# Who copies the dense half tiles, and when the third sequence's z is transposed, in a fused attention and mixture-of-experts kernel

## The chip, the cores and the metric

The kernel runs on one core of a Trainium2 chip. The metric is device time in microseconds (us) of one execution of the whole program, lower is better. The engines are called as in the profile: PE is TensorE (PEld its weight loads), DVE is VectorE, ACT is ScalarE, POOL is GpSimd, SP is SyncE, which here only issues DMAs.

## The reference

```python
B, S, D = u.shape                              # 8, 2816, 256; z has 64 columns
scores = (1 / S) * (z @ z.T)                   # per sequence; symmetric
attn = np.maximum(scores, 0) ** 2
x = (u * (attn @ v)).reshape(B * S, D)         # 22528 tokens
h = np.maximum(x @ w1_dense, 0)                # 512 hidden columns
y_dense = h @ w2_dense
expert = argmax(x @ w_gate)                    # one of 8 experts per token
gate = softmax(x @ w_gate)[expert]
y_moe[token] = gate * (np.maximum(x @ w1[expert], 0) @ w2[expert])
out = y_dense + y_moe
```

## The kernel before, in words

The program has two stages on one core.

**Stage one, attention.** Each of the 8 sequences is 22 blocks of 128 tokens. The columns of A = relu(scores)^2 are made in groups of 2 or 4 blocks, six groups to a sequence: PE computes scores into PSUM (`scores`, L408), ACT or DVE applies relu (L423 or L425) and then the square (L436 or L438), which writes the tile A in SBUF. A has three buffers. Because A is symmetric, some blocks of a group are not computed but taken from an earlier group by a DMA transpose that SP issues (`far_steps`, L493, seen as `A<-A` and `wall<-A`); the buffer of that earlier group can be written again when these transposes have read it. PE then multiplies A by v (`av`, L610), two blocks at a time, and DVE multiplies the result by u (`gate_x`, L637): one L637 per two blocks. DVE also routes (small operations, L681 to L741), and POOL scatters the tokens of a block to per-expert rows in DRAM (L779).

The scores need z transposed. For the first sequence this is done by PE. For every other sequence `turn_z` does it in two halves of 11 blocks: a DVE copy that doubles z (L115, `zn<-zr`) and a DMA transpose on SP's queue (L118, `zT<-zn`). SP's queue is served in order; it also carries the loads of u (L154), the transposes of x for the routing (L639) and those of L493.

The order of the instructions on PE, ACT, DVE and SP is written out when the program is built: a small planner keeps a clock of its own (`now`) and the times at which it believes ACT, DVE and SP's queue to be free, and puts each operation on an engine by these. `tick(g)` is called once per block. `soon(t, fn, dur)` offers a piece of DVE work at tick t with a duration that the planner charges; `issue(1.5)` charges SP's queue for a transpose of z. A group's scores may be started two groups ahead (`ahead`), but those of another sequence only when both halves of its z are in the program (`z_there`).

**Stage two, experts.** The tokens come back from DRAM sorted by expert. The first region has NT1 = 70 tiles of 256 tokens, each tile of one expert; the second region has units of two half tiles of 128 tokens, each half with an expert of its own. A tile is two halves. Per tile, in PE's order (`slot`):

- `up` with the dense weights (L1003, `h_ps<-ring,w1d`, 8 matmuls), and its relu on ACT (L1006)
- `half(s - 2, 1)`: the second half of the tile before the last
- `up` with the expert's weights, and its relu on ACT
- `half(s - 1, 0)`: the first half of the last tile

In between, DVE copies the expert's weights for the next tile to a ring (L990, one copy of 128x2048 per tile in the first region, two per unit in the second). A `half` is: eight matmuls (`down`, L1012) into the tile `y`, four of them for the dense part `y[:, 0]` and four for the expert's part `y[:, 1]`; a copy of the dense part from PSUM to the SBUF tile `yd` by ACT (L1029); one DVE instruction that multiplies the expert's part by the gate, adds `yd` and writes `ys` (L1030); and an indirect DMA from POOL's queue that writes the rows of `ys` to the output (L1032). After some of them POOL does a small copy that only spaces its DMAs (L1017). `y` has two buffers, each a PSUM bank; `h_ps` has three, `yd` three, `ys` nine. PE can write a buffer of `y` again when its L1030 is done. Some of the last scatters of stage one and the tables of the second region (16 steps on DVE, one for each tile from the eleventh on, L821 to L906) are done between the tiles.

Of the kernel before, what the change touches and what calls it, by code (L numbers as in the profile page):

```python
# [19 lines left out]
def kernel(  # L20
# [12 lines left out]
    nc = tc.nc  # L33
# [6 lines left out]
    nK = S // P  # L40
# [9 lines left out]
    NT1 = -(-(Q1 * G * P - E * (T2 - 1)) // T2)  # L50
# [53 lines left out]
    def load_z(b):  # L104
        z_of[b] = zpool.tile([P, nK, dq], BF, name="zr", bufs=1)
        nc.vector.memset(z_of[b][:, 0, 0:1], 0.0)
        nc.gpsimd.dma_start(out=z_of[b][:], in_=z[b].rearrange("(p k) d -> p k d", p=P))

    def turn_z(b, k0, k1):

        if k0 == 0:
            assert not any(left[m] for m in left if groups[m][0] == b - 2)
            zn_of[b] = zpool.tile([P, nK, 2, dq], BF, name="zn", bufs=1)
            zT_of[b] = zpool.tile([P, nK, P], BF, name="zT")
        nc.vector.tensor_copy(  # L115
            zn_of[b][:, k0:k1, :, :],
            z_of[b][:, k0:k1, :].unsqueeze(2).to_broadcast([P, k1 - k0, 2, dq]))
        nc.sync.dma_start_transpose(  # L118
            out=zT_of[b][:, k0:k1, :],
            in_=zn_of[b][:, k0:k1].rearrange("p k h d -> p (k h d)"))  # L120
        issue(1.5)
        if k1 == nK:
            z_there.add(b)

    def load_v(b, h, parts, gate=True):
        if h == 0:
            v_of[b] = zpool.tile([P, nK, D], BF, name="vb")
        src = v[b].rearrange("(p k) d -> p k d", p=P)
        k0, k1 = h * nK // parts, (h + 1) * nK // parts
        if gate:  # L130
            nc.vector.memset(v_of[b][:, k0, 0:1], 0.0)
        nc.gpsimd.dma_start(out=v_of[b][:, k0:k1, :], in_=src[:, k0:k1, :])
        free["pool"] = max(free["pool"], now[0]) + 0.8
# [12 lines left out]
    def issue(dur, ready=0.0):  # L146
        sync[0] = max(sync[0], now[0], ready) + dur
# [114 lines left out]
    def weights(e, half):  # L262
        nc.vector.memset(wall[:, e, half * 2 * F:half * 2 * F + 1], 0.0)
        if half == 0:
            nc.gpsimd.dma_start(
                out=wall[:, e, 0:2 * F].rearrange("p (c f) -> p c f", c=2),
                in_=moe_w1[e].rearrange("(c p) f -> p c f", p=P))
        else:
            nc.gpsimd.dma_start(
                out=wall[:, e, 2 * F:].rearrange("p (c d) -> p c d", c=4),  # L270
                in_=moe_w2[e].rearrange("(c p) d -> p c d", p=P))
# [20 lines left out]
    def offer(ready, rank, ways, then=None):  # L292
        count[0] += 1
        todo.append((rank, count[0], ready, ways, then))
# [120 lines left out]
    def relu(n, ks, s, c, ready, sx):  # L415
# [39 lines left out]
        if n + ks[0] == 0:  # L455
            del ways["act"]
        offer(ready, 1, ways, half)

    def can_turn(n, m):
# [287 lines left out]
    def nodep(ins, mine, *groups_):  # L747
        ins = ins.ins if hasattr(ins, "ins") else ins
        for key in groups_:
            tc.declare_no_dep(ins, group=key, reason="rows of different tokens")  # L750
        for key in mine:
            tc.add_to_no_dep_group(key, ins)
# [3 lines left out]
    def behind(fn):  # L756

        if last_pool:
            with tc.issue_after(last_pool[0]):
                ins = fn()  # L760
        else:
            ins = fn()
        last_pool[:] = [ins.ins]
        return ins
# [172 lines left out]
    def take(name):  # L937
        if not ring:
            rings()
        turn[name] = turn.get(name, -1) + 1  # L940
        return ring[name][turn[name] % len(ring[name])]
# [68 lines left out]
    def down(y, k, h, w2, j):  # L1010
        for f in range(4):
            nc.tensor.matmul(out=y[:, k, :], lhsT=h[:, f, j * P:(j + 1) * P],  # L1012
                             rhs=w2(f), start=(f == 0), stop=(f == 3))

    def pause(src):

        behind(lambda: nc.gpsimd.tensor_copy(take("idle")[:, :src.shape[1]], src))  # L1017
# [3 lines left out]
    def half(s, j):  # L1021

        hd, he, we, me, ids = pend[s]
        we = we[j % len(we)]
        yd, ys = take("yd"), take("ys")
        y = late["y"].tile([P, 2, D], F32, name="yy", tag="y")
        down(y, 0, hd, lambda f: w2d[:, f, :], j)
        down(y, 1, he, lambda f: we[:, 2 * F + f * D:2 * F + (f + 1) * D], j)
        nc.scalar.copy(yd, y[:, 0, :])  # L1029
        nc.vector.scalar_tensor_tensor(out=ys, in0=y[:, 1, :], scalar=me[:, j, 0:1],  # L1030
                                       in1=yd, op0=ALU.mult, op1=ALU.add)
        ins = behind(lambda: nc.gpsimd.indirect_dma_start(  # L1032
            out=out, out_offset=bass.IndirectOffsetOnAxis(ap=ids[j], axis=0),
            in_=ys, in_offset=None, bounds_check=N - 1, oob_is_err=False))
        nodep(ins, ["out"], "out")
        last_row[0] = ins
        if j == 0 and s < NT - MAYBE - 5:
            pause(ys)
# [16 lines left out]
    def slot(s, end):  # L1055

        def second_half():
            if s - 2 in pend:
                if halves(s - 2) == 2:
                    half(s - 2, 1)  # L1060
                del pend[s - 2]
# [33 lines left out]
    def at(tick, fn):  # L1095
        later.setdefault(tick, []).append(fn)

    def soon(t, fn, dur=0.07):
        at(t, lambda: offer(now[0], 3, {"dve": (dur, lambda eng: fn())}))
# [8 lines left out]
    for b in range(B):  # L1108
        t = b * nK
        if b + 1 < B:  # L1110
            soon(max(t - 10, 0), lambda b=b: load_z(b + 1))
            soon(t - 1 if b else 5, lambda b=b: turn_z(b + 1, 0, nK // 2), 0.4)
            soon(t if b else 6, lambda b=b: turn_z(b + 1, nK // 2, nK), 0.4)
            for h in range(2):
                soon(t + (13, 15)[h], lambda b=b, h=h: load_v(b + 1, h, 2))

# [69 lines left out]
    for q in range(nQ - 2):  # L1186
        t = starts[q + 1] - 1 + LAG
# [93 lines left out]
```

## Time and profile before

| what | value |
|---|---|
| three runs | 905.21, 912.65 and 927.82 us, median 912.65 |
| the profiled execution, its own time | 910.9 us |
| its span, first to last instruction | 909.2 us (1.7 us lie around it) |
| mean granted TensorE clock | 0.992 |
| stage one, stage two | about 566 and 343 us of the span |

One execution was profiled. The page gives each engine's busy time and the idle time in front of its instructions with the instruction that ended it ("releaser"). In the views of time each row begins with its start and its duration in us; `x8` is a count of merged instructions, and a bracket at the end says how long the engine sat idle before and what released it. Views by windows give busy time per stretch, with the number of instructions behind an x, then the granted clock (PEclk, 1.00 is full), the share of the DMA engines and GB/s. Ends of matmuls are modelled: eight matmuls of 256 columns are listed with 1.04 us and the next eight begin 0.87 us after them.

### The profile page before, as it was taken

The page shows a single profiled execution, that of the slowest core. Times are in us where ns is not written, and L with a number is a line of the kernel's source. Part 1 is how long each engine was busy: PE and PEld are TensorE (multiplying, and loading weights), DVE is VectorE, ACT ScalarE, POOL GpSimd, SP SyncE. Part 2 cuts the span into 40 slices and gives each one's busy share as a digit, 9 for nine tenths or more (in the row PEclk, how much of TensorE's full clock was granted, in tenths as well). Part 3 has the DMA queues.
Part 4 walks back from the last instruction along what each step waited for, and adds up shares of the span by engine and source line. Part 5 has one row for each costly group of instructions (what it writes and reads, how often), then busy time and mean ns, then how long its engine had stood idle before and what let it go on. Part 6 is the DMA issues. An engine that isn't in the chain of part 4 may idle for free.

```text
span 909.2 us, 30147 instructions
## 1 busy us (share of the span) xinstructions
PE 865.5 (95%) x12178; PEld 757.4 (83%) x12178; DVE 669.7 (74%) x1275; ACT 702.9 (77%) x873; POOL 486.0 (53%) x538
## 2 busy tenths in 40 slices
PE   7999897999999999999999999899999999999996
PEld 5898796898898898788898878688887888888885
DVE  8989695898997998897998985545654444546663
ACT  8989695897897897797897984566766776777664
POOL 7202343244344344344244374778787887777765
PEclk9999999999999999999999999999999999999999
DMA  8998999999999999999999867555544544544333
GB/s 175 174 199 152 179 175 133 172 196 199 194 190 174 200 177 163 192 204 180 200 170 179 148 143 135 118 123 113 113 113 108 115 111 115 112 102 102 92 94 86
DMA packets 289246, 136.80 MB, mean 150 GB/s; under 512 B 258638, under 2 KB 266062, under 8 KB 289104
## 3 DMA queue, kind: packets, MB, share of 16 engines
q1 hardware_dynamic: 263552, 79.40, 52.4%
q0 software_dynamic: 25552, 55.44, 27.4%
q8 instruction: 96, 1.57, 0.7%
q14 instruction: 46, 0.38, 0.1%
HBM read 61.54 MB, written 37.03 MB: 108 GB/s over the span
## 4 chain that ended last, share of the span: by engine, by line
PE 62%; POOL 15%; issue 12%; DVE 5%; DMA 3%; ACT 2%; POOLq 0%; another core or an unknown queue 0%; DVEq 0%; ACTq 0%
PE o L610 41%; POOL out_dram L1032 11%; PE s L408 9%; PE yy L1012 5%; PE h_ps L1003 5%; POOL zr L1017 3%; DMA wall<-A 1%; DVE r L425 1%; PE lg L671 1%; DMA vb<-in_v_dram 1%; ACT A L436 1%; DVE pays L637 1%; DVE ring L1030 1%; DVE A L438 1%; ACT r L423 1%
## 5 line engine op out<-in xcount | busy, mean ns | idle before, releaser
L610 PE MATMUL o<-vb,A 64*128 64x256 bf16 x7184 | 464.4, 270 | 8.5 <-issue 5.8
L610 PEld LDWEIGHTS <-A 64*128 64x128 bf16 x7184 | 381.5, 94 | 51.3 <-issue 10.7
L779 POOL DMA_INDIRECT xs<-pays,pi x176 | 189.1, 1075 | 281.2 <-DVE pi L777 232.5
L423 ACT ACTIVATE r<-s 128x1024 f32<-128x1024 f32 (+1 forms) x246 | 242.5, 1010 | 50.3 <-PE s L408 48.0
L436 ACT ACTIVATE A<-r 128x1024 bf16<-128x1024 f32 (+1 forms) x246 | 248.7, 1042 | 8.7 <-issue 3.1
L1006 ACT ACTIVATE ring<-h_ps 128x1024 bf16<-128x1024 f32 x180 | 184.6, 1026 | 90.8 <-PE h_ps L1003 51.7
L425 DVE TENSOR_SCALAR r<-s 128x1024 f32<-128x1024 f32 x151 | 182.8, 1219 | 14.3 <-PE s L408 12.4
L1030 DVE SCALAR_TENSOR_TENSOR ring<-yy,me,ring 128x256 f32<-128x256 f32 x179 | 86.3, 482 | 141.4 <-ACT ring L1029 70.9
L438 DVE TENSOR_TENSOR A<-r 128x1024 bf16<-128x1024 f32 x145 | 175.3, 1218 | 3.8 <-ACT r L423 2.8
L1032 POOL DMA_INDIRECT out_dram<-ring,me x140 | 145.5, 1039 | 54.9 <-DVE ring L1030 27.2
L1012 PEld LDWEIGHTS <-ring 128*128 128x128 bf16 x1432 | 139.3, 98 | 34.9 <-issue 17.1
L408 PE MATMUL s<-zT 64*128 64x512 bf16 (+1 forms) x874 | 146.9, 357 | 7.7 <-ACT r L423 2.4
L1012 PE MATMUL yy<-w2d,ring 128*128 128x256 bf16 x716 | 107.8, 273 | 12.2 <-DVE ring L1030 11.6
L1012 PE MATMUL yy<-ring 128*128 128x256 bf16 x716 | 107.9, 273 | 2.4 <-ACT ring L1006 1.4
L1003 PE MATMUL h_ps<-ring,w1d 128*128 128x256 bf16 x720 | 93.7, 274 | 2.6 <-ACT ring L1006 2.6
L1003 PE MATMUL h_ps<-ring 128*128 128x256 bf16 (+1 forms) x872 | 93.5, 253 | 0.6 <-ACT ring L1006 0.6
L990 DVE COPY ring<-wall 128x2048 bf16 x109 | 82.9, 775 | 11.6 <-issue 7.1
L637 DVE TENSOR_TENSOR pays<-o,ut 128x512 bf16<-128x512 f32 x88 | 60.2, 684 | 38.7 <-PE o L610 16.9
L1029 ACT COPY ring<-yy 128x256 f32<-128x256 f32 x179 | 67.3, 376 | 23.2 <-PE yy L1012 11.4
L1003 PEld LDWEIGHTS <-ring 128*128 128x128 bf16 x872 | 73.5, 98 | 8.5 <-issue 1.2
L1003 PEld LDWEIGHTS <-w1d 128*128 128x128 bf16 x720 | 70.2, 98 | 11.2 <-issue 2.9
L408 PEld LDWEIGHTS <-zT 64*128 64x128 bf16 x874 | 54.7, 94 | 23.9 <-issue 11.2
(124 smaller groups left out, 448.2 us busy)
## 6 DMA issues: line engine op xcount, KB each, us to landing
ut<-in_u_dram SPq DMA_DIRECT2D x88, 256.0 KB
vb<-in_v_dram POOLq DMA_DIRECT2D x14, 704.0 KB
wall<-in_moe_w_dram POOLq DMA_DIRECT2D x16, 256.0 KB
xs<-pays,pi POOLq DMA_INDIRECT x176
zr<-in_z_dram POOLq DMA_DIRECT2D x7, 352.0 KB
out_dram<-ring,me POOLq DMA_INDIRECT x140
ring<-xs SPq DMA_TRANSPOSE x114
xT<-pays SPq DMA_TRANSPOSE x88
```

What stands on the lines that cost most here:

```text
L408: nc.tensor.matmul(out=s[:, h, y * c:(y + 1) * c], lhsT=zT[r, k + h, :], rhs=zT[r, i0:i0 + w, :], start=True, stop=True)
L423: nc.scalar.activation(r[:, :, :c], s[:, :, :c], AF.Relu, scale=1.0 / S)
L425: nc.vector.tensor_scalar(out=r[:, :, :c], in0=s[:, :, :c], scalar1=1.0 / S, scalar2=0.0, op0=ALU.mult, op1=ALU.max)
L436: nc.scalar.activation(a, r, AF.Square)
L438: (nc.gpsimd if eng == "pool" else nc.vector).tensor_mul(a, r, r)
L610: nc.tensor.matmul(out=o[:, j, 0:D], lhsT=block(n, k, i + j - i0)[r], rhs=v_of[b][r, k, :], start=(p == 0 and x == 0), stop=(p == 1 and x ...
L779: ins = behind(lambda: nc.gpsimd.indirect_dma_start(out=xs, out_offset=bass.IndirectOffsetOnAxis(ap=pi[:], axis=0), in_=pays[:, g % (2 * G ...
L1003: nc.tensor.matmul(out=h_ps[:, f, hs, :], lhsT=w1(c, f), rhs=xT[:, hs, c, :], start=(c == 0), stop=(c == 1))
L1006: nc.scalar.activation(h[:, :, 0:m * P], h_ps[:, :, 0:m, :].rearrange("p f h t -> p f (h t)"), AF.Relu)
L1012: nc.tensor.matmul(out=y[:, k, :], lhsT=h[:, f, j * P:(j + 1) * P], rhs=w2(f), start=(f == 0), stop=(f == 3))
L1030: nc.vector.scalar_tensor_tensor(out=ys, in0=y[:, 1, :], scalar=me[:, j, 0:1], in1=yd, op0=ALU.mult, op1=ALU.add)
L1032: ins = behind(lambda: nc.gpsimd.indirect_dma_start(out=out, out_offset=bass.IndirectOffsetOnAxis(ap=ids[j], axis=0), in_=ys, in_offset=No ...
```

## The change

```diff
@@ half(s, j) @@
-        nc.scalar.copy(yd, y[:, 0, :])
+        if s < NT1:
+            nc.vector.tensor_copy(yd, y[:, 0, :])
+        else:
+            nc.scalar.copy(yd, y[:, 0, :])
         nc.vector.scalar_tensor_tensor(out=ys, in0=y[:, 1, :], scalar=me[:, j, 0:1],
                                        in1=yd, op0=ALU.mult, op1=ALU.add)
@@ the list of what is offered at which tick; t = b * nK, nK = 22 @@
         if b + 1 < B:
             soon(max(t - 10, 0), lambda b=b: load_z(b + 1))
-            soon(t - 1 if b else 5, lambda b=b: turn_z(b + 1, 0, nK // 2), 0.4)
-            soon(t if b else 6, lambda b=b: turn_z(b + 1, nK // 2, nK), 0.4)
+            tz = (5, 6) if b == 0 else (t + 9, t + 11) if b == 1 else (t - 1, t)
+            soon(tz[0], lambda b=b: turn_z(b + 1, 0, nK // 2), 0.4)
+            soon(tz[1], lambda b=b: turn_z(b + 1, nK // 2, nK), 0.4)
```

In the first region (140 half tiles) the copy of the dense part goes from ACT to DVE; in the second region (39 half tiles) it stays on ACT. The two halves of `turn_z` for the third sequence (b = 1) are offered at ticks 31 and 33 in place of 21 and 22; for the other sequences the ticks are as before. Nothing else changes in the source, but the planner sees the moved work at its new place.

## The prediction

> **What bounds the kernel now.** I read the page first, then the windows by stage, then the timelines of the two places that the change touches.
>
> ```profile
> PE 865.5 (95%) x12178; PEld 757.4 (83%) x12178; DVE 669.7 (74%) x1275; ACT 702.9 (77%) x873; POOL 486.0 (53%) x538
> PE 62%; POOL 15%; issue 12%; DVE 5%; DMA 3%; ACT 2%; POOLq 0%; another core or an unknown queue 0%; DVEq 0%; ACTq 0%
> ```
> ```profile
> 0.00:566.00 566.00, 546.65 (x9147) 475.59 (x9148) 485.01 (x885) 472.62 (x513) 226.67 (x242) 0.99 1.02 176
> 586.50:825.40 238.90, 229.66 (x2082) 203.10 (x2080) 123.39 (x244) 167.21 (x261) 187.78 (x216) 1.00 0.48 113
> 825.40:909.20 83.80, 72.91 (x810) 65.45 (x807) 49.74 (x102) 51.46 (x84) 57.10 (x62) 0.98 0.37 92
> ```
>
> The columns after the length are PE, PEld, DVE, ACT and POOL. PE is the bound in all stretches, busy 95% overall and 96% in the first region (second row, tiles 5 to 69). So a change pays only where PE stands still, and costs only where it makes PE stand still. I therefore looked for PE's gaps at the two places.
>
> Place one is the second sequence, ticks 22 to 34:
>
> ```profile
> 86.50 3.72 SPq L118 DMA_TRANSPOSE zT<-zn  x2
> 91.46 2.25 SPq L493 DMA_TRANSPOSE wall<-A  x1
> 95.45 2.22 SPq L493 DMA_TRANSPOSE wall<-A  x1
> 103.25 1.06 ACT L436 ACTIVATE A<-r 128x1024 bf16<-128x1024 f32 x1 [3.04 <-DMA wall<-A]
> 105.27 0.61 PE L408 MATMUL s<-zT 64*128 64x512 bf16 x4 [2.38 <-ACT r L423]
> ```
> ```profile
> 100.00:120.00 20.00, 17.55 (x259) 13.98 (x255) 14.98 (x28) 15.48 (x18) 5.91 (x5) 0.91 0.93 163
> 120.00:140.00 20.00, 19.91 (x364) 18.42 (x360) 17.05 (x31) 16.57 (x20) 10.59 (x12) 1.00 0.99 185
> ```
>
> SP issues the two transposes of the third sequence's z at 86.5, then those of A. The one issued at 95.45 has read its buffer only when ACT goes on at 103.25, so the square that is to overwrite that buffer waits 3.04 us, and PE stands for 2.38 us behind it. The clock of that slice is 0.91: 0.09 of 20 us is 1.8 us more lost.
>
> Place two is a tile of the first region. Undisturbed, tiles begin 3.50 us apart:
>
> ```profile
> 705.57 1.04 PE L1003 MATMUL h_ps<-ring,w1d 128*128 128x256 bf16 x8
> 709.07 1.04 PE L1003 MATMUL h_ps<-ring,w1d 128*128 128x256 bf16 x8
> ```
>
> The window from 586.5 holds 65 tiles in 238.9 us, 3.675 each, so 65 x 0.175 = 11.4 us are lost there. The groups of that window name the waiter:
>
> ```profile
> L1006 ACT ACTIVATE ring<-h_ps 128x1024 bf16<-128x1024 f32 x131 | 135.1, 1031 | 56.8 <-PE h_ps L1003 29.3 <-PE yy L1012 19.5 <-issue 7.7
> L1012 PE MATMUL yy<-w2d,ring 128*128 128x256 bf16 x520 | 77.9, 272 | 9.2 <-DVE ring L1030 8.7 <-issue 0.3
> L1030 DVE SCALAR_TENSOR_TENSOR ring<-yy,me,ring 128x256 f32<-128x256 f32 x131 | 63.3, 483 | 109.7 <-ACT ring L1029 56.5 <-issue 25.7 <-DMA out_dram<-ring,me 10.3
> L990 DVE COPY ring<-wall 128x2048 bf16 x66 | 51.8, 784 | 5.3 <-issue 3.7 <-DVE ring L1030 0.3
> L1029 ACT COPY ring<-yy 128x256 f32<-128x256 f32 x130 | 48.9, 376 | 15.3 <-PE h_ps L1003 7.5 <-PE yy L1012 7.3
> ```
>
> PE waits 8.7 us for L1030 to give back a buffer of `y`, and L1030 waits mostly for the copy. That looks like a case for DVE, but the last row says that the copy itself sat idle 14.8 us for PE: its signal comes late. Two stalls show the two kinds:
>
> ```profile
> 596.90 0.37 ACT L1029 COPY ring<-yy 128x256 f32<-128x256 f32 x1 [1.98 <-PE h_ps L1003]
> 597.84 0.60 PE L1012 MATMUL yy<-w2d,ring 128*128 128x256 bf16 x4 [1.60 <-DVE ring L1030]
> ```
> ```profile
> 752.48 1.02 ACT L1006 ACTIVATE ring<-h_ps 128x1024 bf16<-128x1024 f32 x1 [1.78 <-PE yy L1012]
> 753.40 0.37 ACT L1029 COPY ring<-yy 128x256 f32<-128x256 f32 x1
> 754.39 0.60 PE L1012 MATMUL yy<-w2d,ring 128*128 128x256 bf16 x4 [1.21 <-DVE ring L1030]
> ```
>
> In the first the copy waits for PE with ACT idle: another engine would wait as long. In the second a relu got the late signal and the copy stood 0.92 us behind it: another engine could have begun earlier. Only that kind can be gained.
>
> **Part one: the copy on DVE.** ACT loses 140 x 0.376 = 52.6 us of work, DVE gets 140 copies of 128x256 out of PSUM. None is in the trace; the nearest rows are
>
> ```profile
> L425 DVE TENSOR_SCALAR r<-s 128x512 f32<-128x512 f32 x1 | 0.7, 679 | 0.0
> L729 DVE COPY tb<-pre 128x88 f32<-128x88 f32 x14 | 3.3, 235 | 0.0
> L729 DVE COPY tb<-pre 128x32 f32<-128x32 f32 x2 | 0.4, 182 | 0.1
> ```
>
> The copies rise by 53 ns over 56 columns, 0.95 ns a column; 235 + 168 x 0.95 = 394 ns for 256 columns, the lower end. From L425, which also reads PSUM, 679 - 256 x 0.95 = 436 ns, the upper end. I take 0.40, by the rows of the same operation. So DVE's copy is as long as ACT's (0.376), and what is gained is only the place in the queue.
>
> The gain: of PE's eleven stalls (8.7 us) three have the relu in front, the one shown at 754.39 (1.21 us) and
>
> ```profile
> 689.54 0.60 PE L1012 MATMUL yy<-w2d,ring 128*128 128x256 bf16 x4 [1.02 <-DVE ring L1030]
> 733.80 0.60 PE L1012 MATMUL yy<-w2d,ring 128*128 128x256 bf16 x4 [0.48 <-DVE ring L1030]
> ```
>
> At most 0.92 of each goes: 0.92 + 0.48 + 0.92 = 2.3 us. That holds if the copy's own signal came with the relu's; if it came after the relu's end, as at 596.90, nothing goes. I take half, 1.2 us.
>
> The cost: DVE's queue is in order, and per tile it becomes copy, L1030, L990, copy, L1030.
>
> ```profile
> 716.49 0.76 DVE L990 COPY ring<-wall 128x2048 bf16 x1 [0.22 <-issue]
> 717.21 0.48 DVE L1030 SCALAR_TENSOR_TENSOR ring<-yy,me,ring 128x256 f32<-128x256 f32 x1
> 719.18 0.60 PE L1012 MATMUL yy<-w2d,ring 128*128 128x256 bf16 x4
> 708.52 1.19 DVE L990 COPY ring<-wall 128x2048 bf16 x1
> ```
>
> 2 x (0.40 + 0.48) + 0.22 (the pause ahead of L990) + 0.78 = 2.76 us of 3.50, 79%, where ACT now carries 2 x (1.03 + 0.38) = 2.8. It fits, but the second copy now stands behind L990: copy, L1030, pause and L990 end 0.40 + 0.48 + 0.22 + 0.78 = 1.9 us after the first half's matmuls, while the second half's end 1.75 us after them. So it starts 0.15 us late, 0.55 where L990 takes 1.19. That hides in the slack: L1030 ends at 717.69, PE asks for the buffer at 719.18, 1.49 us later. Where a late signal has used up the slack the delay is PE's: 11 stalls, half of them on a second half, 5.5 x 0.15 = 0.8 us; 11 x 0.55 = 6 us at the worst. Behind the copy wait L1030, the next weights and so PE's next `up`; the table steps of 16 tiles, 0.51 us each by
>
> ```profile
> L871 DVE TENSOR_REDUCE have<-zn 128x44 f32<-128x352 f32 x1 | 0.5, 509 | 0.0
> ```
>
> bring DVE to 2.76 + 0.51 = 3.27 of 3.50, still under. I charge 0.8 us. Part one: -1.2 + 0.8 = **-0.4 us**, bounds -2.3 and +6.
>
> **Part two: z ten blocks later.** It moves two of these copies, 1.74 us of DVE, and the two transposes, 3.72 us of SP's queue:
>
> ```profile
> L115 DVE COPY zn<-zr 128x1408 bf16<-128x1408 bf16 x14 | 12.2, 872 | 0.0
> ```
>
> Without them SP reaches the transposes of A some 3.7 us earlier, more than the 3.04 us that the square waited, so the stall should go. What it is worth I read from the same stretch of the fourth sequence, the outputs (L637) of blocks 20 to 32 against 64 to 76, seven in each window:
>
> ```profile
> 82.00:123.00 41.00, 4.17 (x7) 0.96 1.00 176
> 226.70:264.30 37.60, 4.21 (x7) 1.00 1.10 192
> ```
>
> 41.0 - 37.6 = **3.4 us**; the upper bound is 2.38 + 1.8 = 4.2, the lower a loss of 3 us, if the old stall goes and the new place makes PE wait twice as long (the 3 us below, and the clock). The Trainium skill, page "TensorE: Matmul & The Clock Gate", Part 1, has the clock fall to half only after an idle window of some 3.4 us. By it a gap of 2.38 us would cost no clock and the move would be worth 2.4; the trace differs (0.91), and I keep the trace.
>
> At the new place, about 115 to 126, DVE is busy 15 to 17 of 20 us and takes the copies. SP has transposes of A there:
>
> ```profile
> 113.72 2.79 SPq L493 DMA_TRANSPOSE A<-A  x1
> 120.68 2.64 SPq L493 DMA_TRANSPOSE A<-A  x1
> 128.54 0.40 PE L408 MATMUL s<-zT 64*128 64x256 bf16 x4
> ```
>
> SP's queue waits at each moved transpose for its DVE copy, and behind it stand the loads of u (issued four blocks ahead), the transposes of x and the next one of A. POOL's load of the fourth sequence's z, tick 34, reuses the tile that the copies free at tick 33 instead of 22; it is needed at tick 43, nine blocks on. The deadline is the last row, the first score of the third sequence. Tick 33 comes with the last output of the first window above, near 123: copy by 124, transpose issued by 126. The first scores need the first half only, offered two blocks (some 6 us) earlier. I charge nothing; without that cover PE would wait the 3 us to 128.5 over again.
>
> **Sum.** 910.9 - 0.4 - 3.4 = **907.1 us**. The profiled execution lies 1.75 us under the median of the runs (912.65), inside their scatter, so I leave it there.
>
> **Rivals.** *DVE ends the stalls.* If late signals only cost PE because they pile up on ACT, all 11.4 us of the window go: 910.9 - 11.4 - 3.4 = 896.1. For it: L1030 waits 56.5 us for the copy. Against: the copy's own 14.8 us for PE.
>
> *DVE becomes the bound of the first region* (slower than before). L1030 also waits 10.3 us for output DMAs, and copies behind it now wait too. From 3.50 us of DVE work per tile on, every tile grows: with L990 at 1.19, 2.76 + 0.41 = 3.17, and in the 16 table tiles 3.68, 0.18 x 16 = 2.9 us; the second half's delay at its worst adds 6, and 10.3 us of held copies at 0.4 per wait and six waits 2.4. 910.9 + 11.3 - 3.4 = 918.8. Against: 79% on the mean. A harsher form is that the new copies fight POOL for SBUF, as L990's spread (0.76 to 1.19) suggests for that copy. The Trainium skill, page "GPSIMD Engine Reference", section 1, lets POOL share an SBUF interface with DVE and contend with DVE's two-port modes; "VectorE: DVE Perf Modes" ("Why PSUM operands drop a tier") keeps PSUM sources out of those. No run here shows the new copy; the slope of 0.95 ns agrees.
>
> *The stall only moves.* The transposes of z meet those of A in the fence above, and the next square, or the first score, waits instead: 910.9 - 0.4 = 910.5. For it: 3.72 us come between two transposes that lie 7 us apart and take 2.7 each. Against: the planner charges SP's queue for both and issues those of A by that.
>
> **Chances.** Forecast 0.48 (its own range 903 to 911), DVE ends the stalls 0.20, DVE the bound 0.14, the stall moves 0.13, something else 0.05. The range runs from 895 to 919: it takes in both far cases' centres, leaving about half of each outside. Two per cent of 912.65 is 18 us, about what a measurement of this kernel can tell from no change; only the far side of the first rival reaches it (0.11), and of the second (0.06); 0.83 stays within.
>
> **What would show it.** Right: L1029 on DVE near 400 ns; PE's 2.38 us gap at 105 gone and the slice at 100 back at 1.00; the first region's tiles at 3.66 us with stalls for L1030 still there, after copies that wait for PE. Wrong: tiles near 3.50 (first rival), L990 or the copy named as PE's releaser and tiles over 3.75 (second), a gap of PE between 115 and 135 (third).

## The result, and the profile after

| | before | after |
|---|---|---|
| median of 19 runs each | 912.34 us (903.46 to 927.82) | 924.15 us (914.71 to 938.49) |
| the profiled execution, its span | 910.9, 909.2 | 926.95, 925.2 |
| mean granted clock of it | 0.992 | 0.989 |

The ratio is 1.0125, with a 95% interval of 1.0089 to 1.0161: some 11 us slower, within 2%, and outside the range on record on the slow side. The ratios here and below leave out executions that lie more than 1.5% above the fastest of the same kernel.

The page of the changed kernel, its first part and the chain that ended last, and the windows of stage one, of tiles 5 to 69 and of the rest (columns as before):

```profile
PE 870.0 (94%) x12178; PEld 758.9 (82%) x12178; DVE 729.0 (79%) x1418; ACT 659.3 (71%) x730; POOL 484.3 (52%) x537
PE 72%; POOL 7%; issue 7%; DVE 6%; DMA 5%; ACT 2%; another core or an unknown queue 0%; POOLq 0%; DVEq 0%; ACTq 0%
```
```profile
0.00:572.80 572.80, 547.51 (x9135) 475.54 (x9135) 487.43 (x888) 468.66 (x509) 224.87 (x243) 0.99 1.02 174
595.83:840.06 244.23, 230.61 (x2083) 203.16 (x2081) 175.85 (x369) 130.20 (x131) 185.71 (x212) 1.00 0.46 109
840.06:925.20 85.14, 73.62 (x810) 65.60 (x807) 51.01 (x106) 50.66 (x80) 58.59 (x63) 0.98 0.36 91
```

The copies did move: DVE has 59 us more, ACT 44 less. DMA is now 5% of the chain, where it was 3%. Stage one ends, by the first matmul of tile 0, at 572.79 instead of 564.67; these are the row of before and the row of after:

```profile
564.67 1.05 PE L1003 MATMUL h_ps<-ring,w1d 128*128 128x256 bf16 x8
```
```profile
572.79 1.05 PE L1003 MATMUL h_ps<-ring,w1d 128*128 128x256 bf16 x8
```

So the 16.0 us between the two spans are 8.1 in stage one, 1.2 in tiles 0 to 4 (23.0 against 21.8), 5.3 in tiles 5 to 69 (244.2 against 238.9, or 3.757 a tile against 3.675) and 1.3 behind them. Half of the loss is in the stage in which I had booked the gain. PE's gaps there, in the timeline of PE:

```profile
125.91 0.38 PE L408 MATMUL s<-zT 64*128 64x256 bf16 x3 [0.30 <-DVE pays L637]
130.36 0.39 PE L408 MATMUL s<-zT 64*128 64x256 bf16 x1 [4.07 <-DMA zT<-zn]
224.65 1.04 PE L408 MATMUL s<-zT 64*128 64x512 bf16 x4 [4.34 <-DVE wall L263]
364.39 0.61 PE L408 MATMUL s<-zT 64*128 64x512 bf16 x4 [2.56 <-DVE pi L777]
```
```profile
100.00:120.00 20.00, 20.00 (x337) 17.03 (x333) 19.23 (x37) 19.15 (x22) 5.74 (x6) 1.00 1.07 175
```

The gap of 2.38 us at 105 is gone, as forecast: the slice from 100 has PE busy throughout, at full clock. Three new gaps come for it, 11 us together. They are not all loss: the profiled execution of the kernel before has one more gap, longer than the one at 105, that the forecast did not name and whose cause the profile doesn't show:

```profile
154.16 1.50 PE L610 MATMUL o<-vb,A 64*128 64x256 bf16 x13 [4.64 <-issue]
```

It is absent after the change. Gaps of 1 us and more between 20 us and the end of stage one sum to 7.0 us before and 12.0 after. With the half clock behind them (two stretches of 3.41 us before; 3.41, 6.83 and 3.41 us after, by the record of the granted clock) that is most of the 8.1 us.

The first of the new gaps waits for the moved zT. SP's timeline shows its two transposes:

```profile
118.95 1.93 SPq L118 DMA_TRANSPOSE zT<-zn  x1
120.93 1.14 SPq L154 DMA_DIRECT2D ut<-in_u_dram  x1
122.12 1.21 SPq L639 DMA_TRANSPOSE xT<-pays  x1
123.42 2.79 SPq L118 DMA_TRANSPOSE zT<-zn  x1
```

They were issued when I had said, by 126; but the first scores come in sets of four matmuls over four neighbouring blocks of zT, the third set reads blocks 8 to 11, and block 11 lies in the second half. Three of its matmuls ran at 125.91; the fourth waited for that half, which landed 4 us after its issue had ended. The other two gaps name a DVE instruction as releaser that had itself been held up. DVE's timeline at these places:

```profile
223.90 0.69 DVE L637 TENSOR_TENSOR pays<-o,ut 128x512 bf16<-128x512 f32 x1 [5.17 <-DMA xs<-pays,pi]
353.79 0.69 DVE L637 TENSOR_TENSOR pays<-o,ut 128x512 bf16<-128x512 f32 x1 [4.37 <-DMA xs<-pays,pi]
363.65 0.69 DVE L637 TENSOR_TENSOR pays<-o,ut 128x512 bf16<-128x512 f32 x1 [3.79 <-DMA xs<-pays,pi]
```

`pays` holds 22 blocks. L637 writes two of them and must wait until the scatters (L779) of the blocks 22 earlier have read theirs. No L637 of stage one waits for a scatter in the profiled execution of the kernel before. Nothing in the change touches scatters.

In the first region (lines of tiles 5 to 69):

```profile
L1006 ACT ACTIVATE ring<-h_ps 128x1024 bf16<-128x1024 f32 x131 | 131.6, 1023 | 115.8 <-PE h_ps L1003 64.8 <-PE yy L1012 40.3 <-ACT ring L1006 5.4
L1012 PE MATMUL yy<-w2d,ring 128*128 128x256 bf16 x520 | 77.9, 272 | 13.5 <-DVE ring L1033 12.0 <-issue 1.2
L1030 DVE COPY ring<-yy 128x256 f32<-128x256 f32 x130 | 54.6, 420 | 53.8 <-PE h_ps L1003 25.0 <-PE yy L1012 23.2 <-issue 4.8
L990 DVE COPY ring<-wall 128x2048 bf16 x65 | 53.2, 818 | 5.8 <-issue 5.1
```

L1030 is now the copy and L1033 what was L1030. The copy takes 420 ns and still sits idle for PE. PE's stalls for L1033 are 12.0 us where they were 8.7.

### The profile page after: what moved, and what is told of

The parts are those of the page before. It is cut to its first block, busy times and chain, and to the rows that moved or that the text cites. A ratio compares the mean times of both kernels' runs of the same rounds, so it can differ in the third digit from the quotient of the medians.

```text
span 925.2 us, 30146 instructions
## 1 busy us (share of the span) xinstructions
PE 870.0 (94%) x12178; PEld 758.9 (82%) x12178; DVE 729.0 (79%) x1418; ACT 659.3 (71%) x730; POOL 484.3 (52%) x537
## 4 chain that ended last, share of the span: by engine, by line
PE 72%; POOL 7%; issue 7%; DVE 6%; DMA 5%; ACT 2%; another core or an unknown queue 0%; POOLq 0%; DVEq 0%; ACTq 0%
PE o L610 37%; PE yy L1012 13%; PE h_ps L1003 12%; PE s L408 8%; POOL out_dram L1035 5%; DMA xs<-pays,pi 3%; DVE r L425 1%; ACT A L436 1%; PE lg L671 1%; DVE ring L1033 1%; ACT r L423 1%; POOL zr L1017 1%; DMA vb<-in_v_dram 1%; DVE ring L1030 1%; DMA zT<-zn 1%
## 5 line engine op out<-in xcount | busy, mean ns | idle before, releaser
L779 POOL DMA_INDIRECT xs<-pays,pi x176 | 187.1, 1063 | 291.2 <-DVE pi L777 242.2
L1006 ACT ACTIVATE ring<-h_ps 128x1024 bf16<-128x1024 f32 x180 | 180.7, 1020 | 151.5 <-PE h_ps L1003 84.5
L423 ACT ACTIVATE r<-s 128x1024 f32<-128x1024 f32 x245 | 242.0, 1015 | 59.9 <-PE s L408 58.6
L425 DVE TENSOR_SCALAR r<-s 128x1024 f32<-128x1024 f32 (+1 forms) x152 | 182.5, 1209 | 13.7 <-PE s L408 12.7
L438 DVE TENSOR_TENSOR A<-r 128x1024 bf16<-128x1024 f32 x147 | 178.1, 1221 | 0.8
L1033 DVE SCALAR_TENSOR_TENSOR ring<-yy,me,ring 128x256 f32<-128x256 f32 x179 | 86.4, 483 | 30.7 <-ACT ring L1032 12.5
L1030 DVE COPY ring<-yy 128x256 f32<-128x256 f32 x140 | 58.8, 420 | 58.9 <-PE yy L1012 25.3
L637 DVE TENSOR_TENSOR pays<-o,ut 128x512 bf16<-128x512 f32 x88 | 60.4, 686 | 49.5 <-PE o L610 14.1
L990 DVE COPY ring<-wall 128x2048 bf16 x109 | 84.7, 791 | 13.2 <-issue 9.1
```

The source lines that it names most:

```text
L423: nc.scalar.activation(r[:, :, :c], s[:, :, :c], AF.Relu, scale=1.0 / S)
L425: nc.vector.tensor_scalar(out=r[:, :, :c], in0=s[:, :, :c], scalar1=1.0 / S, scalar2=0.0, op0=ALU.mult, op1=ALU.max)
L438: (nc.gpsimd if eng == "pool" else nc.vector).tensor_mul(a, r, r)
L779: ins = behind(lambda: nc.gpsimd.indirect_dma_start(out=xs, out_offset=bass.IndirectOffsetOnAxis(ap=pi[:], axis=0), in_=pays[:, g % (2 * G ...
L1006: nc.scalar.activation(h[:, :, 0:m * P], h_ps[:, :, 0:m, :].rearrange("p f h t -> p f (h t)"), AF.Relu)
```

## The experiments

Edits are to the kernel before unless said otherwise; each was timed against it in the same rounds. In these rounds the kernel before takes 873 to 876 us, not 912 (they ran on three chips, which agree; on which chip the first set ran is not on record, so whether the chip makes the difference stays open). PE's late signals hardly occur in them, and the first region runs without a stall (the window of tiles 5 to 69 of a kernel, "lost", whose stage two is that of before: 227.07 us, 3.493 a tile, PE busy 227.07 of them). So these runs can't tell what the copy does behind late signals.

```profile
572.45:799.52 227.07, 227.07 (x2082) 203.53 (x2080) 121.10 (x241) 167.29 (x261) 186.58 (x220) 1.00 0.56 122
```

**Each part alone.** Letters name theories, those after A where an expectation first brings them up. Theory A at the start: both parts lose and add. R1: the copy is the loss. R2: z's wait is. R3: the scatter waits have nothing to do with the scatters' lead.

The kernel copy_only has the first part of the change's diff, z_only the second:

```diff
-        nc.scalar.copy(yd, y[:, 0, :])
+        if s < NT1:
+            nc.vector.tensor_copy(yd, y[:, 0, :])
+        else:
+            nc.scalar.copy(yd, y[:, 0, :])
```
```diff
+            tz = (5, 6) if b == 0 else (t + 9, t + 11) if b == 1 else (t - 1, t)
-            soon(t - 1 if b else 5, lambda b=b: turn_z(b + 1, 0, nK // 2), 0.4)
-            soon(t if b else 6, lambda b=b: turn_z(b + 1, nK // 2, nK), 0.4)
+            soon(tz[0], lambda b=b: turn_z(b + 1, 0, nK // 2), 0.4)
+            soon(tz[1], lambda b=b: turn_z(b + 1, nK // 2, nK), 0.4)
```

> Only the copy of the first region goes to VectorE; z stays where it was. Theory A (two causes that add: about 8 us in stage one from z, about 7 us in the first region and its ends from the copy): ratio 1.006 to 1.008, tiles of the first region at 3.74 to 3.78 us, stage one as before (ends near 564). Rival R1 (the copy is the whole loss, the new gaps of stage one are chance of one execution): ratio 1.012 to 1.015. Rival R2 (the copy is neutral, z is the whole loss): ratio 0.998 to 1.002.

> Only z of the third sequence is moved by ten blocks; the copy stays on ScalarE. Theory A: ratio 1.005 to 1.009, stage one ends near 572, with PE's waits near 130 (4 us, for zT), 224 (4 us) and 364 (2.6 us, both behind a VectorE output L637 that waits for a scatter), tiles at 3.67. R1: ratio 1.000 and no such waits. R2: ratio 1.012.

> The changed kernel itself once more, beside the kernel with z moved alone. Theory B (the loss is z's; the copy on VectorE costs only where PE's signals come late): if the tiles of the first region run at 3.49 us, the ratio is that of z alone, 1.009 to 1.018; if they run at 3.6 or more, the copy adds 5 us and the ratio is 1.012 to 1.02. Rival (the copy is the loss): well above z alone on either chip.

Measured: the copy alone 0.9973 (0.9938 to 1.0008), z alone 1.0146 (1.0092 to 1.0200), the changed kernel itself 1.0117 (1.0079 to 1.0154). The product of the first two is 1.0119. In these rounds the copy is not the loss; z is all of it that can be measured. With the copy on DVE the region takes 227.39 us and PE has no stall in it:

```profile
574.33:801.72 227.39, 227.28 (x2082) 203.40 (x2080) 175.26 (x374) 132.99 (x131) 187.37 (x222) 1.00 0.53 122
L1030 DVE COPY ring<-yy 128x256 f32<-128x256 f32 x131 | 55.3, 422 | 40.4 <-PE yy L1012 39.0
```

R1 falls, and the first half of theory A with it; what is left is z, as R2 has it, though not yet why.

**How much room DVE has.** The copy made twice, one behind the other:

```diff
+        if s < NT1:
+            nc.vector.tensor_copy(yd, y[:, 0, :])
+            nc.vector.tensor_copy(yd, y[:, 0, :])
```

> z as before; VectorE makes the copy of the first region twice, one after the other, so VectorE has 0.84 us more per tile than in the change. With one copy VectorE waits 39 of the region's 227 us for PE's yy; the second copy takes 55. If VectorE has only that slack, the region grows by some 16 us: tiles at 3.70 to 3.78, ratio 1.016 to 1.024, PE waits for L1033. If the slack is larger (the queue overlaps more than its rows show): tiles under 3.6.

Measured: 1.0193 (1.0151 to 1.0235). The region:

```profile
569.49:809.42 239.93, 233.76 (x2080) 202.81 (x2080) 223.19 (x505) 132.62 (x130) 184.77 (x218) 1.00 0.47 114
L1012 PE MATMUL yy<-w2d,ring 128*128 128x256 bf16 x520 | 77.8, 272 | 6.1 <-DVE ring L1034 3.8 <-DVE ring L1031 0.7
```

3.691 us a tile. The second copy is 54 us of DVE work by its own rows; DVE's busy time in the region rises by 48, since neighbouring rows overlap. The region is 12.5 us longer, between the 9 and the 15 by which these exceed the 39 us for which DVE had waited. One copy fits, two don't; DVE's 79% was room.

**Theory A's second half: the scatters' lead.** One scatter is offered per tick. In the planner's own times the places of the second group were ready at 100.3, ahead of tick 29 at 100.7; with z moved they are ready at 101.8, behind tick 29 at 101.6. So that tick sends nothing, and every later scatter runs a block later: in the traces a scatter is issued some 9 us (median) ahead of the L637 that needs its buffer, where it was some 11.5. Two kernels, z_catch (z_only and the first edit, in `tick`) and lost (the second alone):

```diff
         one_scatter()
+        if g == 30:
+            one_scatter()
```
```diff
-        one_scatter()
+        if g != 29:
+            one_scatter()
```

> z moved as above, and one scatter more is offered at tick 30, so that the scatters catch up the one block that they lost at tick 29, where the second group's places were not ready. Theory A: the scatters run 11 us ahead of the buffer's next use instead of 8.5, so the waits of L637 for scatters near 224 and 364 go, and the wait for zT near 130 stays: 6.9 us of gaps and some 3 us of half clock less than z_only, ratio 0.995 to 1.000. Rival R3 (the waits of L637 come from the loads of v on the same queue whatever the lead, or from other changes of the order): the same as z_only.

> The kernel before with nothing moved, but no scatter is offered at tick 29, so that all later scatters run one block later. Theory A: VectorE's L637 waits for scatters near 220 and 360 as in the changed kernel, 6 to 10 us more, ratio 1.006 to 1.011; PE's old gap of 2.38 us near 105 stays. R3, and R2 (the wait for zT is the loss): ratio 1.000, no such waits.

Measured: z_catch 1.0087 (1.0047 to 1.0126), lost 0.9997 (0.9958 to 1.0036). The profiled execution of "lost" does show such waits, this one and one of 4.71 us at 343.35, with gaps of PE of 3.00 and 2.41 us behind them:

```profile
214.99 0.69 DVE L637 TENSOR_TENSOR pays<-o,ut 128x512 bf16<-128x512 f32 x1 [4.40 <-DMA xs<-pays,pi]
```

but its runs are not slower. A lost block makes such waits possible and costs nothing by itself that can be measured: theory A falls as the cause. Whether the caught-up block wins back some of z_only's 1.0146, or none as R3 has it, can't be told: the intervals of the two overlap.

**z at other places.** z57 has the line below, z57_catch the caught-up scatter too, z13 has (t + 1, t + 3) there, z_early (t - 3, t - 2); z_early_v is z_only with the last line.

```diff
+            tz = (5, 6) if b == 0 else (t + 5, t + 7) if b == 1 else (t - 1, t)
```
```diff
-                soon(t + (13, 15)[h], lambda b=b, h=h: load_v(b + 1, h, 2))
+                soon(t + ((2, 4) if b == 1 else (13, 15))[h], lambda b=b, h=h: load_v(b + 1, h, 2))
```

> z of the third sequence is transposed at ticks 27 and 29 instead of 31 and 33 (copy on ScalarE): both halves are there four blocks before the first scores of that sequence, but the scatters still lose the block of tick 29. Theory B (two parts: the wait for zT of 2.6 to 6.3 us with its half clock, and the lost block, worth some 5 us together with it): no wait for zT near 130, some waits of L637 for scatters left, ratio 1.000 to 1.006. Rival (any place after tick 22 costs the same, since the order of the rest changes): 1.012 to 1.016.

> As the last, and one scatter more is offered at tick 30, so that the lead of the scatters is back at 11 us. Theory B: neither wait, and the old gap of 1 to 2.4 us near 105 gone too: ratio 0.994 to 1.000, clock 0.997 or more. Rival (the order of the rest): 1.008 to 1.012, as with the late z and the caught-up scatter.

> z of the third sequence at ticks 23 and 25: the place of tick 29 is not lost, and zT is early. Theory B: 0.995 to 1.002; the gap near 105 may stay, since the two transposes of z still stand ahead of those of A in SP's queue. Rival (any later place): 1.008 or more.

> The other way: z of the third sequence at ticks 19 and 20 instead of 21 and 22, away from the transposes of A (copy on ScalarE). Theory C and D: the old gap near 105 goes and nothing comes for it, ratio 0.994 to 0.999. Rival (any change of the order costs): 1.003 or more.

> z moved by ten blocks as in the change (copy on ScalarE), but v of the third sequence is loaded at ticks 24 and 26 instead of 35 and 37, away from z's new place; no block of scatters is lost here. Theory C: PE's wait for zT near 130 shrinks under 2 us and no L637 waits for a scatter between 135 and 160, ratio 1.000 to 1.004. Theory D: the wait for zT stays at 2.6 us or more, ratio 1.007 to 1.012, as with the caught-up scatter.

Measured: z57 1.0063 (1.0022 to 1.0104), z57_catch 1.0134 (1.0093 to 1.0175), z13 1.0031 (0.9994 to 1.0069), z_early 1.0197 (1.0155 to 1.0240), z_early_v 1.0195 (1.0142 to 1.0248). Theory B expected the middle places to win: it falls with z57_catch, for which it had 0.994 to 1.000; z13 can't be told from no change. A place two ticks *earlier* than before costs 2%, where theories C and D had 0.994 to 0.999; no deadline explains that. z_early_v lies above what either theory had for it, and its trace has the longest wait of PE for zT of all, 10.65 us, up to 141.69.

**The traffic.** Transposes of z repeated at the change's place, into a buffer that is free:

```diff
+    def again(b, k0, k1):
+        nc.sync.dma_start_transpose(
+            out=w2d[:].rearrange("p f d -> p (f d)").rearrange("p (k q) -> p k q", q=P),
+            in_=zn_of[b][:, k0:k0 + 8].rearrange("p k h d -> p (k h d)"))
+        issue(1.5)
...
+            if b == 1:
+                soon(t + 9, lambda b=b: again(b + 1, 0, nK // 2), 0.07)
+                soon(t + 11, lambda b=b: again(b + 1, nK // 2, nK), 0.07)
```

> The kernel before with z where it was; at ticks 31 and 33, where the change puts the transposes, SP issues two more transposes of 8 of z's 22 blocks each into the buffer of w2d, which is free until tick 40 and is overwritten by its load then. So the transfers come late as in the change, but nothing waits for them and no scatter is lost. Theory C (transposes at this place crowd the queues of transfers just ahead of the loads of z and v, and the scatters behind those land late): waits of VectorE's L637 for scatters between 135 and 160, ratio 1.004 to 1.010. Theory D (the change loses by its deadline and by the order that follows from it, not by the traffic): 0.998 to 1.002.

Measured: 1.0084 (1.0050 to 1.0117), as theory C had it, but its profile has no wait of L637 for a scatter. The `issue(1.5)` of the repeated transposes had also changed the planner's order, so it tells nothing apart.

**Taking traffic or speed away.** The pause, in `scores` of z_only and of z57_catch; z_only with half of the third sequence's v; and, in `turn_z`, no z of the third sequence at all:

```diff
+        if (n, ks[0]) == (9, 18):
+            for x in range(12):
+                r = slice(x % 2 * dq, (x % 2 + 1) * dq)
+                nc.tensor.matmul(out=s[:, x % 2, 0:c], lhsT=zT[r, ks[0] + x % 2, :],
+                                 rhs=zT[r, i0:i0 + w, :], start=True, stop=True)
```
```diff
-            for h in range(2):
+            for h in range(1 if b == 1 else 2):
...
+            if b == 1:
+                soon(t + 15, lambda: nc.gpsimd.memset(v_of[2][:, nK // 2:, :], 0.0))
```
```diff
+        if b == 2:
+            zT_of[b] = zT_of[1]
+            if k1 == nK:
+                z_there.add(b)
+            return
```

> z moved by ten blocks alone, and in the scores of group 9, blocks 18 and 19 (near 100 us) TensorE repeats 12 matmuls of 64x512, some 2.5 us of work that changes no value: about the 2.4 us for which PE stood at 105 in the kernel before. Theory F (the gap at 105 let the queues of transfers drain; with it gone PE runs ahead and pays later, in larger waits): the added work is won back, ratio 1.000 to 1.010. Theory D (deadline and order): the added work adds, ratio 1.014 to 1.018.

> The same 12 repeated matmuls in the kernel with z at ticks 27 and 29 and the caught-up scatter. Theory F: ratio 0.998 to 1.006, less than the 1.013 without them. Theory D: 1.012 to 1.018.

> z moved by ten blocks alone; the second half of the third sequence's v, 704 KB at tick 37, is not loaded, GpSimd writes zeros there instead (so that part of v is left out). Theory C (transfers crowd here: z's transposes, the loads of z and v, the scatters behind them on one queue): no wait of L637 for a scatter between 135 and 160, ratio 1.002 to 1.010, the wait for zT near 130 stays. Theory D: 1.012 or more, since deadline and order are the same.

> The third sequence's z is neither copied nor transposed, its scores use the second sequence's zT (so its values are left out): all traffic and all waits of these transposes are gone, and the gap at 105 with them. If a z placed ideally could win anything, this is the most that it wins. My sum on record, 3.4 us, gives 0.995 to 0.998. Theory F: the gap at 105 goes and later waits come for it, 0.998 to 1.008. Rival (any change of the order costs): 1.006 or more.

Measured: 1.0132 (1.0073 to 1.0191), 1.0205 (1.0156 to 1.0253), 1.0108 (1.0065 to 1.0150) and 1.0140 (1.0074 to 1.0206). Theory F falls: a pause wins nothing back that can be told, and in z57_catch it costs. Half of v gives 1.0108, between what C and D expected: inconclusive. The deadline half of theory D falls: a kernel that has no z to wait for loses as much as z_only. Work was taken away, and the kernel got slower. Of D only the order is left.

**The order of the rest.** What all the kernels share that lose by a moved or missing z is that the planner, whose clock the move shifts, writes a new order for the stretch behind it. PE's list has 24,564 weight loads and matmuls. Counted are the lines removed and added in the shortest list of differences from that of before, with an operation named by its tiles, offsets and shapes and the buffers of a ring taken as one: copy_only and copy_twice 0, lost 80, dup 1,928, and those with z moved or left out 1,140 to 1,214 (the repeated matmuls of the pauses not counted). In the changed kernel the first 2,546 operations are as before, and all but 8 of the 187 places that differ lie ahead of operation 8,911, some 86 to 280 us; behind that PE is back in the old order. (The expectation of z_same_order below speaks of 25 thousand lines of the rest of stage one; by this count it is 1,204, nearly all between 86 and 280 us.) So: move the transposes, or leave them out, and let the planner book them where they were.

```diff
-        issue(1.5)
+        if b != 2:
+            issue(1.5)
...
+            soon(t - 1 if b else 5, lambda b=b: turn_z(b + 1, 0, nK // 2) if b != 1 else issue(1.5), 0.4)
+            soon(t if b else 6, lambda b=b: turn_z(b + 1, nK // 2, nK) if b != 1 else issue(1.5), 0.4)
+            if b == 1:
+                at(t + 9, lambda b=b: turn_z(b + 1, 0, nK // 2))
+                at(t + 11, lambda b=b: turn_z(b + 1, nK // 2, nK))
```

That is z_same_order. no_z_same_order is no_z with `issue(1.5)` kept ahead of its return. By the same count PE's, ACT's and POOL's lists are then those of before to the line; DVE's and SP's differ by the moved (or missing) operations alone.

> z of the third sequence is copied and transposed at ticks 31 and 33 as in the change, but the planner books it at ticks 21 and 22 as before: the orders of PE, ScalarE and GpSimd are then word for word those of the kernel before, and of VectorE's and SP's only the two copies and the two transposes move. Theory E (the loss comes from the new order that the planner writes for the rest of stage one, 25 thousand lines of PE's list, not from the transposes): the wait for zT near 130 may show, the waits of L637 for scatters do not, ratio 0.997 to 1.006. Theory C (the transfers at the new place): 1.008 or more, with waits of L637 near 140 to 157.

> The third sequence's z is neither copied nor transposed and its scores use the second sequence's zT (its values are left out), and the planner books them as before, so that PE's, ScalarE's and GpSimd's orders are word for word those of the kernel before. Theory E: the gap near 105 is gone or shorter and nothing comes for it, ratio 0.993 to 1.000, against 1.014 with the order written anew. Theory C and F (transfers, or PE running ahead of them): 1.004 or more.

Measured: z_same_order 0.9982 (0.9940 to 1.0023), no_z_same_order 1.0022 (0.9992 to 1.0053). With the order kept, the same transposes at the same place cost nothing, and leaving them out wins nothing. Theory E stands, and C falls by z_same_order. For no_z_same_order E had 0.993 to 1.000; the measured 1.0022 lies between that and the 1.004 from which C and F begin, far from no_z's 1.0140. Another rival is that not the order costs the time but the other buffers that the same operations get with it. "lost" speaks against it: with buffers told apart PE's list differs there by 16,486 lines, in z_only by 13,796, and "lost" costs nothing.

The windows of 100 to 120 and 120 to 160 us show what happens, first z_only, then z_same_order, then no_z, then no_z_same_order (one execution each; those of z_only, 896.3 us, and z_same_order, 883.0 us, are among the longest of their kernels):

```profile
100.00:120.00 20.00, 20.00 (x337) 17.05 (x335) 19.25 (x36) 19.38 (x22) 5.89 (x6) 1.00 1.06 186
120.00:160.00 40.00, 27.51 (x459) 22.86 (x455) 20.57 (x45) 18.65 (x21) 11.57 (x14) 0.93 1.21 136
```
```profile
100.00:120.00 20.00, 20.00 (x335) 16.81 (x331) 18.68 (x36) 18.13 (x20) 6.92 (x7) 1.00 1.06 192
120.00:160.00 40.00, 39.30 (x679) 35.09 (x677) 36.23 (x66) 34.57 (x39) 18.60 (x19) 1.00 1.11 197
```
```profile
100.00:120.00 20.00, 19.98 (x329) 16.95 (x327) 18.91 (x34) 19.57 (x22) 7.90 (x6) 1.00 0.98 178
120.00:160.00 40.00, 33.71 (x533) 27.81 (x530) 24.67 (x53) 23.11 (x26) 14.03 (x16) 0.91 1.12 127
```
```profile
100.00:120.00 20.00, 20.00 (x335) 17.07 (x333) 19.37 (x34) 19.42 (x22) 7.90 (x7) 1.00 1.11 187
120.00:160.00 40.00, 39.91 (x694) 35.81 (x690) 35.89 (x65) 34.72 (x39) 17.75 (x19) 1.00 1.10 183
```

In all of them PE runs through 100 to 120 without the old gap. In the 40 us after that PE is busy 27.5 and 33.7 us with the new order, 39.3 and 39.9 with the old one. A PE that stands asks for fewer transfers; but the DMA engines are as busy in z_only and no_z (1.21 and 1.12) as in the other two (1.11 and 1.10), and move 136 and 127 GB/s where those move 197 and 183. So in these two the transfers themselves take longer.

The other profiled executions of these rounds agree, with two exceptions. With the old order (also copy_only, copy_twice and "lost") PE is busy for 39.3 to 39.9 of the 40 us. With a new one it is 26.3 to 34.6 in ten kernels of twelve, and as much as with the old in z13 (39.5) and z57_catch:

```profile
120.00:160.00 40.00, 39.91 (x697) 35.09 (x693) 34.06 (x65) 33.31 (x37) 16.92 (x19) 1.00 1.11 190
```

That execution of z57_catch took 876.8 us, the shortest of its six, whose median is 887.15. So a new order does not lose this time in every execution. Nor does the old one always keep it: in the first set the profiled execution of the kernel before, with the gap at 154, has PE busy for 34.7 there. PE's gaps in z_only, and behind the largest the scatter that DVE waited for:

```profile
128.27 0.28 PE L408 MATMUL s<-zT 64*128 64x256 bf16 x1 [2.60 <-DMA zT<-zn]
157.92 0.61 PE L408 MATMUL s<-zT 64*128 64x512 bf16 x2 [7.30 <-DVE pays L637]
```
```profile
157.17 0.69 DVE L637 TENSOR_TENSOR pays<-o,ut 128x512 bf16<-128x512 f32 x1 [8.58 <-DMA xs<-pays,pi]
```
```profile
137.08 0.98 POOL L779 DMA_INDIRECT xs<-pays,pi  x1 [0.30 <-issue]
```

That L637 writes blocks 40 and 41 and needs the scatter of block 19, the last row: 20 us from issue to landing. In z_same_order PE's only gap between 95 and 160 is

```profile
128.46 0.39 PE L409 MATMUL s<-zT 64*128 64x256 bf16 x4 [0.59 <-DVE vb L132]
```

The wait for zT is gone too: in the old order PE comes to the second half of zT late enough (the third set of scores starts at 130.22, in the changed kernel at 125.91).

What in the new orders slows the transfers, and why not in every execution, stays open. Twelve kernels with such an order were timed, with z at some place or absent: ratios from 1.0031 to 1.0205, eleven of them with the whole interval above 1, and no single wait is common to their traces. None of the runs beats the kernel before by more than its interval; copy_only and z_same_order come nearest, and both together were not run.

## Why the prediction was wrong

**What bounds the kernel; the two places.** Right for the two places. The gap at 105 was z's transposes ahead of those of A in SP's queue: with the order kept and z moved or gone, it is gone. The forecast missed the longer gap at 154 (4.64 us). No profiled execution of copy_only, copy_twice or "lost" has it, so it may be chance.

**Part one, -0.4 us.** Right in mechanism and size, as far as runs show it: the copy takes 420 ns (0.40 forecast), the copy alone gives 0.9973, -2.4 us of 873 with an interval of -5.4 to +0.7. The delay behind L990 hid in the slack, as argued; copy_twice shows where the slack ends. What was not isolated is the copy behind late signals: there one execution of each kernel gives 3.757 against 3.675 us a tile, and that 5.3 us, near the +6 that I had as the worst, may be the copies or chance. The changed kernel's ratio was 1.0125 there and 1.0117 here: 0.7 us apart, with some 5 of uncertainty, so 5.3 us is neither shown nor excluded.

**Part two, -3.4 us: the step that failed.** I costed it as a move of "two of these copies, 1.74 us of DVE, and the two transposes, 3.72 us of SP's queue" and left all other work where it was. The text ahead of the forecast says that a planner writes the order by its clock, and that `soon` and `issue` charge it; I used that only as an argument against a rival. A move of a charged step is a new order of what follows, here of 1,204 lines of PE's list behind its first 2,546 operations, removed and added counted. Priced by itself, the move is -1.6 us (interval -5.2 to +2.0), so the sign of the local sum may even be right; the new order is worth some +14 (1.0146 against 0.9982, of 874). That the order is the cause is shown by the two pairs, z_only and z_same_order, no_z and no_z_same_order; how it slows the transfers is not.

**The deadline, "I charge nothing".** Wrong in the changed kernel: 4.07 us at 130. I took "the first scores need the first half only" for a cover of six microseconds, and the third set of four matmuls already reads the second half. With the old order it was right: no gap waits for zT.

**The rivals.** DVE ends the stalls: no, the tiles did not fall to 3.50. DVE becomes the bound: no, by copy_only, where signals come in time; POOL's contention with the copy doesn't show in its mean: 422 ns with POOL busy 187 of 227 us, inside the 394 to 436 of the forecast. The rule of the Trainium skill, "GPSIMD Engine Reference", section 1, which the forecast set beside this rival, changes nothing here that the runs show. The stall only moves: this names the gap at 130, but its 910.5 was far too low, since it too counted one wait and no new order.

**The range** was built from local bounds; none of its cases held a reordering, so its upper end, 919, had no term for what happened.

## What to carry to other kernels

Where a program plans the order, compare the emitted lists of instructions before pricing an edit: if they differ beyond the edit, the edit is a new schedule and a sum of local terms doesn't price it. Compare them by operation, with the buffers of a ring taken as one, or renamed buffers hide where the order really changes. To learn what the edit itself is worth, book it in the planner where it was and move only the instructions. Here the edit alone was worth nothing that can be measured and the new schedule 14 us, and even leaving work out lost when it came with a new order.

## What the hardware showed

- A gap of PE halves its clock at less than the 3.4 us of idle time that the Trainium skill, "TensorE: Matmul & The Clock Gate", Part 1, gives. Between 20 and 560 us of the 20 traces, by their record of the granted clock, 29 of 30 gaps of 2.63 us or more brought a half clock of 3.41 us or a multiple of it (the other fell within one; eight of the 30 are shorter than 3.4), five of eight between 2.38 and 2.61, one of 14 between 1.3 and 2.2. The median clock of the runs was 0.996 for the kernel before and 0.990 for z_only in the same rounds: 0.006 x 880 = 5.3 us, three such periods (1.7 us lost in each).
- At a DMA share above 1.0 the engines moved between 114 (z_early, at 1.07) and 197 GB/s (z_same_order, at 1.11) in the 40 us from 120 on, and in z_only a scatter landed 20 us after its issue.
- The same program took 912 us in one set of runs and 873 in the others. In the profiled executions at hand ("lost" stands for before, with the same stage two) 12 us of that are tiles 5 to 69, where PE's signals come late in the first set and don't in the others.
